# GpSimd ops that wait for the VectorE op ahead of them on a shared SBUF access, in a windowed attention and MLP kernel

## The chip, the cores and the metric

The kernel runs on one core of one Trainium2 chip. The metric is the device time of one execution in microseconds (us), as the median of a few runs. The names in this text: PE is TensorE (PEld its weight loads), DVE is VectorE, ACT is ScalarE, POOL is GpSimd, SP is the engine that issues the DMAs. "L399" is line 399 of the kernel file.

## The reference

Attention over 4 batches, 8 heads, 768 positions of 64 elements, in which a query sees the first 8 keys and the 96 keys up to itself, with a slope per head on the distance. Its output, 3072 tokens of 512, goes through a two-layer network with a cosine gate. All is float32.

```python
scores = scale * np.matmul(q, k.transpose(0, 1, 3, 2)) - slopes * dist
scores = np.where(keep, scores, -1000000000.0)      # keep: is_global | is_local
a = np.exp(scores - np.max(scores, axis=-1, keepdims=True))
a = a / (np.sum(a, axis=-1, keepdims=True) + 1e-09)
x = np.matmul(a, v)                                 # then heads side by side: 3072 x 512
h = x @ w_in                                        # 512 -> 2048
return (h * np.cos(h)) @ w_out                      # 2048 -> 512
```

The network's two weights arrive as float64, so the kernel gets them as pairs of 32-bit words and makes float32 of them itself.

## The kernel before

**Tiling.** The tokens are cut into 8 chunks of 384 (half a batch). A chunk's attention is done in 4 units of two heads (`plan_unit`, `plan_values`): scores on PE (L521 in the first 8 units, L525 later), a masked fold (L538) and the minimum of each row (L547) on DVE, the exponentials on ACT (L572), sums and reciprocals on DVE (L580, L583), the normalisation (`norm`, L595 and L600) on DVE or POOL, transposes on PE (L664), masking on the way out of PSUM on DVE (L672, L677), the product with the values on PE (L699). The result is split into a high and a low part, xh (L253 on ACT or L255 on DVE, the helper `copy`) and xl (L720, DVE).

**The network.** It goes in steps of 128 of the 2048 hidden columns (`plan_step`): PE multiplies by a block of w_in (L735, three products for the high and low parts), ACT and DVE make h cos h in four ops that hand on to each other (L752 ACT, L755 DVE, L758 ACT, L793 DVE), the result is split into gh (`copy`) and gl (L802, DVE or POOL), and PE multiplies by a block of w_out (L746). Two PSUM banks take turns for the first product.

**The weights.** Each of the 32 blocks of 128 x 512 weights goes through six ops (`plan_weights`): `wlow` (L378 on ACT, L380 on DVE or POOL), `wsign` (L385 on DVE, L388 on POOL), `wbias` (L394 ACT, L396 DVE or POOL), `wjoin` (L399, DVE only), `whigh` (`copy`: L253 ACT, L255 DVE, L257 POOL) and `wrest` (L409, DVE or POOL). The first 8 blocks of each weight are wanted for the first chunk, the others for the second (`PHASES`). Their raw words stay in tiles of their own; the joined words pass through two tiles `wu`.

**The order.** `Plan.run` goes through time with a cost in ns for each op on each engine it may run on, and picks an engine and a place in its queue. Ops with `port=True` on DVE, and every op on POOL, share one access to SBUF in this plan: `self.port` is the time until which it is taken, and the plan starts no second op on it before that. So in the plan's own times a POOL op and a marked DVE op are never under way together. What the plan gives out is a list of ops by start, and `emit` writes them into the engines' queues in that list's order. What each instruction waits for on the chip is what its data and buffers ask, and its own queue.

```python
holds = lambda o, x: x == POOL or (x == DVE and o.port)
...
if held and holds(o, e):
    continue
```

Until 45 us of the plan's time `emit` also fills PE's gaps with products of zeros (L1039).

Of the kernel before, what the change touches and what calls it, by code (L numbers as in the profile page):

```python
# [40 lines left out]
PE, ACT, DVE, POOL, SP = "PE", "ACT", "DVE", "POOL", "SP"  # L41
# [34 lines left out]
class Op:  # L76
    def __init__(self, engines, emit, after, uses, due, table, extra, port, mode):
        self.engines, self.emit, self.uses, self.due, self.table = engines, emit, uses, due, table
        self.extra, self.port, self.mode = extra, port, mode
        self.after = [a for a in after if a is not None]  # L80
        self.then = []
        self.left = len(self.after)
        self.ready = 0
        self.start = None


class Plan:
# [17 lines left out]
    def op(self, engines, emit, after=(), uses=(), due=None, table=None, extra=0, port=False, mode=None):  # L105
        o = Op(engines, emit, after, list(uses), due, table, extra, port, mode)
        for a in o.after:
            a.then.append(o)
        for u in o.uses:
            u.users += 1  # L110
        self.ops.append(o)
        return o
# [120 lines left out]
class Net:  # L233
# [789 lines left out]
    def emit(self, ops, banks):  # L1023

        nc = self.nc
        held = {b: [] for b in banks}
        for u in {id(u): u for o in ops for u in o.uses if u.at in held}.values():
            held[u.at].append((u.begin, u.end))
        last = 0
        for o in ops:  # L1030
            if o.engine == PE and o.start < FILL_TO:
                each = FILL_EACH if last > FILL_COLD else 2 * FILL_EACH
                n = int((o.start - last - FILL_REST) / each) if last else FILL_FIRST
                free = [b for b in banks if all(y < last or x > o.start for x, y in held[b])]
                if n > 0 and free:
                    ps = self.psum.tile([P, 512], F32, name="idle", tag=free[0])
                    wide = self.zeros.rearrange("p (o w) -> p o w", o=1).broadcast_to([P, 4, P])
                    for _ in range(n):
                        nc.tensor.matmul(ps, self.zeros, wide, start=True, stop=True)  # L1039
                last = o.start + o.engines[PE]  # L1040
            o.emit(o.engine)


def build(tc, *args):
# [54 lines left out]
```

## Time and profile before

| | |
|---|---|
| median of 3 runs | 712.63 us (712.12 to 714.5) |
| the profiled execution, its own time | 714.17 us |
| its span, first to last instruction | 712.4 us |
| PE busy | 688.6 us, 97% |
| DVE busy | 518.8 us, 73% |
| ACT busy | 450.9 us, 63% |
| POOL busy | 135.8 us, 19%, 166 instructions |
| mean granted clock of PE | 0.991 |

A share here is a mean over unlike stretches: PE's gaps lie almost all in the first 57 us and in the last 10, and POOL's work lies almost all in the first 160 us, where it makes the weights. The timeline gives each instruction's start and duration, and in brackets the idle time before it and what ended it.

### The profile page before, as it was taken

The page shows a single profiled execution, that of the slowest core. Times are in us where ns is not written, and L with a number is a line of the kernel's source. Part 1 is how long each engine was busy: PE and PEld are TensorE (multiplying, and loading weights), DVE is VectorE, ACT ScalarE, POOL GpSimd, SP SyncE. Part 2 cuts the span into 40 slices and gives each one's busy share as a digit, 9 for nine tenths or more (in the row PEclk, how much of TensorE's full clock was granted, in tenths as well). Part 3 has the DMA queues.
Part 4 walks back from the last instruction along what each step waited for, and adds up shares of the span by engine and source line. Part 5 has one row for each costly group of instructions (what it writes and reads, how often), then busy time and mean ns, then how long its engine had stood idle before and what let it go on. Part 6 is the DMA issues. An engine that isn't in the chain of part 4 may idle for free.

```text
span 712.4 us, 12947 instructions
## 1 busy us (share of the span) xinstructions
PE 688.6 (97%) x4483; PEld 598.4 (84%) x4483; DVE 518.8 (73%) x1542; ACT 450.9 (63%) x1130; POOL 135.8 (19%) x166
## 2 busy tenths in 40 slices
PE   7898999999999999999999999999999999999996
PEld 3657878988888888889889898888888888899884
DVE  7999999898767778487775887667785877743332
ACT  5799977786756576466664667566764666634342
POOL 4715656530002121011000121011000112000000
PEclk8999999999999999999999999999999999999999
DMA  8997210022420322132230422203122310001001
GB/s 303 407 351 209 59 48 24 1 59 64 112 68 29 83 65 65 48 103 60 56 71 15 112 61 58 59 19 106 42 68 67 90 49 2 1 1 45 1 0 50
DMA packets 32603, 55.74 MB, mean 78 GB/s; under 512 B 3472, under 2 KB 18192, under 8 KB 32528
## 3 DMA queue, kind: packets, MB, share of 16 engines
q1 hardware_dynamic: 32528, 54.82, 26.4%
q8 instruction: 37, 0.61, 0.4%
q14 instruction: 38, 0.31, 0.1%
HBM read 48.52 MB, written 6.29 MB: 77 GB/s over the span
## 4 chain that ended last, share of the span: by engine, by line
PE 72%; DVE 11%; ACT 8%; issue 2%; DMA 1%; POOL 0%; ACTq 0%; DVEq 0%; POOLq 0%; SPq 0%
PE bank L735 31%; PE bank L746 30%; PE bank L699 5%; PE bank L525 3%; ACT tt L572 2%; PE bank L664 2%; DVE wu L399 1%; ACT rr L758 1%; ACT L572 1%; DVE w L409 1%; DVE tt L547 1%; DVE gl L802 1%; DVE rr L755 1%; DVE qs L623 1%; DMA raw<-in_qk_dram 1%
## 5 line engine op out<-in xcount | busy, mean ns | idle before, releaser
L735 PE MATMUL bank<-xh,w 128*128 128x384 f32 x1024 | 298.1, 343 | 4.3 <-DVE rr L793 4.3
L746 PE MATMUL bank<-w,gh 128*128 128x512 f32 x768 | 243.6, 398 | 0.0
L735 PEld LDWEIGHTS bank<-xh,w 128*128 128x128 f32 x1024 | 189.1, 189 | 12.0 <-DVE rr L793 5.8
L735 PE MATMUL bank<-xl,w 128*128 128x384 f32 x512 | 173.3, 339 | 0.8 <-DVE xl L720 0.8
L746 PEld LDWEIGHTS bank<-w,gh 128*128 128x128 f32 x768 | 138.4, 188 | 21.5 <-ACT raw L394 0.3
L746 PE MATMUL bank<-w,gl 128*128 128x512 f32 x384 | 151.9, 396 | 0.0
L755 DVE SCALAR_TENSOR_TENSOR rr<-rr,bank 128x384 f32<-128x384 int32 x129 | 69.8, 542 | 102.6 <-ACT rr L752 102.2
L752 ACT ACTIVATE rr<-bank 128x384 int32<-128x384 f32 x129 | 62.1, 482 | 127.5 <-PE bank L735 124.5
L758 ACT ACTIVATE rr<-rr,half_pi 128x384 f32<-128x384 f32 x129 | 78.4, 613 | 43.0 <-DVE rr L755 41.4
L735 PEld LDWEIGHTS bank<-xl,w 128*128 128x128 f32 x512 | 96.8, 189 | 5.4 <-DVE xl L720 1.4
L793 DVE TENSOR_TENSOR rr<-bank,rr 128x384 f32<-128x384 f32 x129 | 70.5, 551 | 41.2 <-ACT rr L758 40.6
L572 ACT ACTIVATE tt<-tt,st 96x104 f32<-96x104 f32 (+1 forms) x256 | 94.2, 369 | 7.0 <-DVE st L547 6.4
L746 PEld LDWEIGHTS bank<-w,gl 128*128 128x128 f32 x384 | 72.1, 188 | 16.7
L257 POOL TENSOR_SCALAR ks<-raw 128x408 fp32r<-128x408 f32 (+1 forms) x35 | 21.1, 602 | 308.6 <-PE bank L525 291.6
L802 DVE TENSOR_TENSOR gl<-rr,gh 128x384 fp32r<-128x384 f32 (+1 forms) x113 | 65.9, 583 | 7.7 <-ACT gh L253 5.5
L253 ACT CAST gh<-rr 128x384 fp32r<-128x384 f32 (+1 forms) x99 | 50.2, 508 | 29.0 <-DVE rr L793 20.5
L547 DVE CUSTOM_DVE_ANT_0 tt<-bank,dd 96x104 f32<-96x104 f32 (+1 forms) x256 | 55.7, 257 | 3.0
L699 PEld LDWEIGHTS bank<-pv,v 104*64 104x64 f32 (+1 forms) x960 | 42.1, 138 | 12.5 <-issue 8.0
L525 PEld LDWEIGHTS bank<-ks,qs 128*96 128x96 f32 x384 | 45.8, 162 | 5.3 <-issue 0.8
L699 PE MATMUL bank<-pv,v 104*64 104x96 f32 (+1 forms) x960 | 48.3, 252 | 0.8 <-DMA raw<-in_qk_dram 0.4
L525 PE MATMUL bank<-ks,qs 128*96 128x200 f32 (+1 forms) x384 | 47.9, 255 | 0.5 <-DVE st L547 0.5
L572 ACT ACTIVATION_READ_ACCUMULATOR tt<-tt,st 96x1 f32 x256 | 47.9, 187 | 0.0
(96 smaller groups left out, 727.0 us busy)
## 6 DMA issues: line engine op xcount, KB each, us to landing
raw<-in_qk_dram SPq DMA_DIRECT2D x48, 224.0 KB
raw<-in_qk_dram SPq DMA_DIRECT2D x48, 198.0 KB
raw<-in_w_in_dram SPq DMA_DIRECT2D x16, 512.0 KB
raw<-in_w_out_dram SPq DMA_DIRECT2D x16, 512.0 KB
out_dram<-oo SPq DMA_DIRECT2D x24, 256.0 KB
v<-in_v_dram SPq DMA_DIRECT2D x16, 240.0 KB
v<-in_v_dram SPq DMA_DIRECT2D x16, 192.0 KB
raw<-in_qk_dram SPq DMA_DIRECT2D x4, 448.0 KB
```

Of the source, the lines that this page charges most:

```text
L253: self.nc.scalar.copy(out, x)
L525: nc.tensor.matmul(out, qs[:, m, q0], ks[:, k : k + w], start=m == 0, stop=m == 1)
L547: nc.vector.tensor_tensor_reduce(tt[t // 2].tile[:, t % 2, j, :w], ps.tile[:R, i * WIN : i * WIN + w], self.dd[:, v, :w], op0=ALU.add, op1 ...
L572: nc.scalar.activation(x, x, AF.Exp, bias=st.tile[:, c : c + 1], scale=-1.0, accum_out=st.tile[:, n2 + c : n2 + c + 1])
L699: nc.tensor.matmul(px.tile[j * D : (j + 1) * D, t * R : (t + 1) * R], vs.tile[:k, t + c, hs][:, j * D : (j + 1) * D], pv[:k, c, o : o + R] ...
L735: self.nc.tensor.matmul(ph[:, :CW], self.wi[f][:, w, kk * P : (kk + 1) * P], xx[:, kk, :], start=kk == 0 and m == 0, stop=kk == self.NK - ...
L746: self.nc.tensor.matmul(po, gg[:, ts], self.wo[f][:, w, :], start=start and m == 0, stop=stop and m == 2)
L752: self.nc.scalar.activation(r.bitcast(I32), ph, AF.Copy, scale=1.0 / TWO_PI, bias=0.25)
L755: self.nc.vector.scalar_tensor_tensor(r, r.bitcast(I32), -TWO_PI, ph, op0=ALU.mult, op1=ALU.add)
L758: self.nc.scalar.activation(r, r, AF.Sin, bias=self.half_pi)
L793: {DVE: dve}, lambda e, r=r, h=h: nc.vector.tensor_tensor(r(), h(), r(), op=ALU.mult), [o], [ph, rr]
L802: self.eng(e).tensor_tensor(g[1][:, cs], r(), g[0].bitcast(F32)[:, cs], op=ALU.subtract)
```

## The change

`emit` keeps the last instruction of the last DVE op with `port=True`, and the next POOL op in the list gets a wait on it. Each such DVE op is waited for at most once: a second POOL op right behind gets no wait of its own, but stands behind the first in POOL's queue. DVE never waits for POOL because of this change. The `norm`, `krest`, `low`, `wlow`, `wsign`, `wbias`, `whigh` and `wrest` ops on POOL are touched.

```diff
+        held_by = None
+        behind = mybir.DependencyInfo(mybir.DependencyClass.Sync, mybir.DependencyReason.SCHED_ONLY)
         for o in ops:
...
+            new = len(nc.cur_bb.bb.instructions)
             o.emit(o.engine)
+            if o.engine in (DVE, POOL):
+                engine = self.eng(o.engine).engine
+                new = [i for i in nc.cur_bb.bb.instructions[new:] if i.engine == engine]
+                if o.engine == DVE and o.port:
+                    held_by = new[-1]
+                elif o.engine == POOL and held_by is not None:
+                    self.tc.add_manual_dep(new[0], held_by.name, behind, reason="port")
+                    held_by = None
```

No instruction changes its place in any queue. What differs is the waits. POOL's queue at the start of the program, from the first scaling of queries (`raw_158`) on; `DVE_49` is DVE's semaphore, `DMAHW…` those of the loads:

```order
-L490 TENSOR_SCALAR raw_158<-raw_158,steep_104 128x384 [waits DMAHW3_49]
-L380 TENSOR_SCALAR raw_120<-raw_120 128x512 [waits DMAHW1_49]
+L490 TENSOR_SCALAR raw_158<-raw_158,steep_104 128x384 [waits DMAHW3_49,DVE_49]
+L380 TENSOR_SCALAR raw_120<-raw_120 128x512 [waits DMAHW1_49,DVE_49]
 L388 TENSOR_SCALAR raw_120<-raw_120 128x512 [waits Pool_49]
 L595 TENSOR_TENSOR tt_258<-tt_258,st_259 96x2x96 [waits DVE_49,Activation_49]
 L595 TENSOR_TENSOR tt_258<-tt_258,st_259 96x208 [waits Activation_49]
-L388 TENSOR_SCALAR raw_122<-raw_122 128x512 [waits DMAHW3_49,Activation_49]
+L388 TENSOR_SCALAR raw_122<-raw_122 128x512 [waits DMAHW3_49,DVE_49,Activation_49]
 L380 TENSOR_SCALAR raw_124<-raw_124 128x512 [waits DMAHW4_49]
 L490 TENSOR_SCALAR raw_229<-raw_229,steep_104 128x384 [waits DMAHW6_49,PE_49]
```

The first `wlow` and the next block's `wsign` now wait for DVE; the ops between keep their waits.

POOL's queue a little later, the weights' blocks that it reaches between 28 and 51 us:

```order
-L388 TENSOR_SCALAR raw_121<-raw_121 128x512 [waits DMAHW7_49]
+L388 TENSOR_SCALAR raw_121<-raw_121 128x512 [waits DMAHW7_49,DVE_49]
 L388 TENSOR_SCALAR raw_128<-raw_128 128x512 [waits DMAHW1_49,Activation_49]
-L380 TENSOR_SCALAR raw_131<-raw_131 128x512 [waits DMAHW1_49]
-L380 TENSOR_SCALAR raw_133<-raw_133 128x512 [waits DMAHW2_49]
-L388 TENSOR_SCALAR raw_130<-raw_130 128x512 [waits DMAHW3_49,Activation_49]
-L409 TENSOR_TENSOR w_759<-wu_755,w_759 128x512 [waits Activation_49]
+L380 TENSOR_SCALAR raw_131<-raw_131 128x512 [waits DMAHW1_49,DVE_49]
+L380 TENSOR_SCALAR raw_133<-raw_133 128x512 [waits DMAHW2_49,DVE_49]
+L388 TENSOR_SCALAR raw_130<-raw_130 128x512 [waits DMAHW3_49,DVE_49]
+L409 TENSOR_TENSOR w_759<-wu_755,w_759 128x512 [waits DVE_49,Activation_49,Pool_49]
```

Each of these but one has got a wait for DVE of its own; where that wait implies an older one, the older one is gone.

The same queue where the second half of the weights is made, some 120 to 135 us into the run:

```order
-L388 TENSOR_SCALAR raw_150<-raw_150 128x512 [waits DMAHW4_49]
-L409 TENSOR_TENSOR w_1594<-wu_1585,w_1594 128x512 [waits Activation_49]
-L388 TENSOR_SCALAR raw_145<-raw_145 128x512
-L409 TENSOR_TENSOR w_1640<-wu_1633,w_1640 128x512 [waits Activation_49]
-L388 TENSOR_SCALAR raw_147<-raw_147 128x512 [waits DMAHW7_49]
+L388 TENSOR_SCALAR raw_150<-raw_150 128x512 [waits DMAHW4_49,DVE_49]
+L409 TENSOR_TENSOR w_1594<-wu_1585,w_1594 128x512 [waits Activation_49,Pool_49]
+L388 TENSOR_SCALAR raw_145<-raw_145 128x512 [waits DVE_49]
+L409 TENSOR_TENSOR w_1640<-wu_1633,w_1640 128x512 [waits Activation_49,Pool_49]
+L388 TENSOR_SCALAR raw_147<-raw_147 128x512 [waits DMAHW7_49,DVE_49]
```

A `wsign` here waited for nothing but its data, long there; it now waits for DVE.

Which DVE op each waits for is told by the count in the built program. 65 of POOL's ops wait for a later DVE op than before. Laid on the trace of before, 45 of these 65 started there before that DVE op had ended: 9 of them in the first 57 us, 23 from 57 to 160 us, 13 later. The ones that matter most, with times of the trace of before:

| POOL op, its start | the DVE op it now waits for, its end |
|---|---|
| L380 at 11.27 | L600, 13.71 |
| L388 at 18.88 | L600, 20.38 |
| L388 at 21.59 | L399, 27.00 |
| L388 at 28.11 | L385, 36.94 |
| L380 at 31.28 | L399, 40.87 |
| L380 at 32.55 | L409, 43.16 |
| L388 at 33.28 | L399, 47.42 |
| L632 at 80.66 | L583, 83.26 |
| L632 at 97.40 | L399, 101.97 |
| L388 at 99.54 | L399, 104.48 |
| L409 at 109.17 | L255, 110.87 |
| L388 at 111.93 | L409, 115.25 |
| L802 at 313.50 | L623, 314.97 |

## Rows read from the trace of the kernel before

**Rows 1.** The page, part 1: busy time, share of the span and instructions.
```profile
PE 688.6 (97%) x4483; PEld 598.4 (84%) x4483; DVE 518.8 (73%) x1542; ACT 450.9 (63%) x1130; POOL 135.8 (19%) x166
```
**Rows 2.** Busy time by stretch: length, each engine's busy us, PE's granted clock, DMA share.
```profile
20.00:57.00 37.00, 30.30 (x243) 19.24 (x242) 36.10 (x125) 33.58 (x99) 17.02 (x18) 1.00 1.04 379
57.00:160.00 103.00, 100.55 (x650) 86.73 (x651) 94.36 (x224) 82.70 (x186) 57.57 (x47) 0.98 0.22 55
14.00:18.00 4.00, 4.00 (x21) 2.04 (x22) 3.47 (x20) 2.58 (x9) 0.09 (x1) 0.50 1.03 407
```
**Rows 3.** Timeline of PE: start, duration of the row, idle before and what ended it.
```profile
13.86 0.85 PE L664 MATMUL bank<-ident,tt 96*104 96x96 f32 x4 [1.08 <-DVE tt L600]
...
35.03 0.57 PE L664 MATMUL bank<-ident,tt 96*96 96x96 f32 x4 [1.34 <-ACT raw L378]
...
56.84 0.44 PE L735 MATMUL bank<-xh,w 128*128 128x384 f32 x1 [3.70 <-DVE rr L793]
...
102.49 0.44 PE L735 MATMUL bank<-xl,w 128*128 128x384 f32 x1 [0.83 <-DVE xl L720]
...
114.24 0.44 PE L735 MATMUL bank<-xh,w 128*128 128x384 f32 x1 [0.63 <-DVE rr L793]
...
316.42 1.39 PE L699 MATMUL bank<-pv,v 96*64 96x96 f32 x28 [0.41 <-DVE pv L677]
```
**Rows 4.** Timeline of DVE in the first 57 us.
```profile
11.26 1.08 DVE L595 TENSOR_TENSOR tt<-tt,st 96x192 f32<-96x192 f32 x2
12.27 1.44 DVE L600 TENSOR_TENSOR tt<-tt,st 96x416 f32<-96x416 f32 x1
...
17.36 0.16 DVE L580 TENSOR_SCALAR st<-st 96x8 f32<-96x8 f32 x1
...
18.63 1.75 DVE L600 TENSOR_TENSOR tt<-tt,st 96x416 f32<-96x416 f32 x1
20.68 0.56 DVE L720 TENSOR_TENSOR xl<-bank,xh 128x384 fp32r<-128x384 f32 x1 [0.30 <-ACT xh L253]
...
23.80 0.67 DVE L580 TENSOR_SCALAR st<-st 96x8 f32<-96x8 f32 x1
...
25.27 0.64 DVE L595 TENSOR_TENSOR tt<-tt,st 96x192 f32<-96x192 f32 x2
25.82 0.58 DVE L600 TENSOR_TENSOR tt<-tt,st 96x416 f32<-96x416 f32 x1
26.32 0.68 DVE L399 SCALAR_TENSOR_TENSOR wu<-raw 128x512 uint32<-128x512 uint32 x1
...
29.72 0.55 DVE L672 TENSOR_TENSOR pv<-bank,others 104x384 f32<-104x384 f32 x1
...
32.66 1.09 DVE L399 SCALAR_TENSOR_TENSOR wu<-raw 128x512 uint32<-128x512 uint32 x1
33.67 1.50 DVE L595 TENSOR_TENSOR tt<-tt,st 96x192 f32<-96x192 f32 x2
...
36.20 0.74 DVE L385 TENSOR_SCALAR raw<-raw 128x512 uint16<-128x512 uint16 x1
```
**Rows 5.** Timeline of POOL.
```profile
12.20 1.33 POOL L388 TENSOR_SCALAR raw<-raw 128x512 bf16<-128x512 bf16 x1
...
28.11 2.50 POOL L388 TENSOR_SCALAR raw<-raw 128x512 bf16<-128x512 bf16 x2
...
33.28 1.66 POOL L388 TENSOR_SCALAR raw<-raw 128x512 bf16<-128x512 bf16 x1
...
83.41 0.88 POOL L600 TENSOR_TENSOR tt<-tt,st 96x416 f32<-96x416 f32 x1 [1.68 <-DVE st L583]
```
**Rows 6.** Timeline of ACT, the `wbias` behind the `wsign` at 28.11.
```profile
38.11 0.67 ACT L394 ACTIVATE raw<-raw 128x512 f32<-128x512 f32 x1
```
**Rows 7.** Timeline of DVE from 97 to 115 us.
```profile
99.80 1.57 DVE L409 TENSOR_TENSOR w<-wu,w 128x512 fp32r<-128x512 f32 x1
...
112.16 1.56 DVE L399 SCALAR_TENSOR_TENSOR wu<-raw 128x512 uint32<-128x512 uint32 x1
```

## The prediction, made before the changed kernel ran

> **What bounds the kernel now.** Read the page's first part first [rows 1]: PE is busy 97% of the span, so at most some 24 us of PE's time can be won at all, and POOL, the one engine whose instructions change, is busy 19%. Then look where PE stands idle, by stretches [rows 2]. From 57 to 160 us PE idles 103 - 100.55 = 2.45 us. Before 57 us it waits much more, and part of what it does there is products of zeros. In that early stretch DVE is the full engine: 36.10 of 37 us from 20 to 57. So the time until PE runs without gaps is set by how fast DVE gets through its queue, and from then on by PE itself. Last, the timeline of PE [rows 3] says what ends its gaps: 3.70 us before 56.84, after which it is dense, and smaller ones at 13.86, 35.03, 102.49, 114.24 and 316.42. DVE stands behind all of them. The 1.34 us before 35.03 are put down to an old ACT op, but the two L595 there write what that transpose reads, so I take them as the cause.
>
> What has POOL to do with it? The same DVE op is long where a POOL op is under way and short where none is [rows 4]: L600 takes 0.58 us at 25.82, and 1.44 at 12.27 beside POOL's L388 of 12.20 [rows 5]; the two L595 take 0.64 together at 25.27, and 1.08 and 1.50 beside POOL; L399 takes 0.68 at 26.32 and 1.09 at 32.66. Ops that read PSUM don't care: L672 at 29.72 takes 0.55 in the middle of the two L388 of 28.11. POOL is there at that moment only because it runs ahead of the plan, by up to 14 us (the L388 at 33.28, for which the wait would end at 47.42).
>
> **The change part by part.** No instruction is added to an engine's work and none moves in a queue, DMAs included; POOL issues none. What is added is waits on POOL.
>
> *Startup, what DVE gets back.* In the first 57 us, the ops of POOL that moved leave these DVE ops alone: L595 at 11.26, 1.08 - 0.64 = 0.44; L600 at 12.27, 1.44 - 0.58 = 0.86; L580 at 23.80, 0.67 - 0.16 (as at 17.36) = 0.51; L399 at 32.66, 1.09 - 0.68 = 0.41; L595 at 33.67, 1.50 - 0.64 = 0.86. Sum 3.08 us. The L600 at 18.63 is long too (1.75), but the DVE op of 20.68 waited 0.30 us for ACT, which waits for PE: what L600 gains there only lengthens that wait, so I count nothing; it is the upper bound, 1.75 - 0.58 = 1.17 more. Do the moved POOL ops hit other DVE ops instead? After most of the DVE ops waited for, DVE's queue has PSUM work for longer than POOL needs; one L380 (behind the L409 that ends at 43.16) has less room than it needs. Its price lies between 0 and the 0.41 that an L380 cost L399 at 32.66; I take the middle, 0.2. So DVE arrives 2.9 us earlier where PE becomes dense; the lower bound is 0.
>
> *Startup, who waits for the late POOL ops.* The L388 that now waits until 36.94 ends 1.33 us later at 38.27; the `wbias` L394 that needs it started at 38.11 [rows 6]. It slips by some 0.2 us on ACT, and DVE reads it later still. The L388 of 21.59 has three ops behind it in POOL's queue; they all start after 27.00, and even at 1.33 us each the four end by 32.32, before the L399 of 32.66 that reuses a buffer of theirs. Both hold because DVE's own place in the plan is what POOL waits for; I charge nothing.
>
> *From 57 us on.* PE is dense, so only its gaps count. The 0.83 us before 102.49 wait for an L720 that stands behind an L409 of 1.57 us [rows 7] (0.68 by L399, another two-input op of the same size); the 0.63 before 114.24 for an L793 behind an L399 of 1.56. Both are longer by more than the gap, and the POOL ops beside them (99.54, 111.93) now wait. I take both gaps as gone: 1.46 us. At 313.50 POOL's L802 starts just ahead of L623, and the 0.41 us before 316.42 follow; the pattern comes once more 167 us later, so 0.82. Lower bound 0 for each; upper bound the 2.45 us of the whole stretch and these.
>
> *A cost.* The normalisation L600 of POOL at 83.41 now stands behind an L632 that waits for 83.26 and takes 1.06; it starts about 84.4 in place of 83.41, and a transpose on PE wants it. Price between 0 and 1.0; I take 0.3, since PE has other work queued ahead of that transpose.
>
> *Sum.* 2.9 + 1.46 + 0.82 - 0.3 = 4.9 us. The profiled execution took 714.17 us (span 712.4), so 709.3 for such a one; it lies 1.54 above the median, so **707.7 us** against 712.63. A measurement of this kernel can tell about 0.3% (2.1 us) from no change.
>
> *A rule against it.* In the row, L600 (12.27 to 13.71) ends 0.18 us after the L388 beside it (12.20 to 13.53) and takes 0.58 alone, so it is held for most of L388's time and not for all of it. The Trainium skill (SBUF — State Buffer, section "SBUF: two separate sides") says that VectorE and GpSimd share a port pair as an exclusive lock, and that whichever starts first has it while the other blocks fully. The trace agrees in kind, not in the full length. By that rule alone a wait ahead of the lock wins nothing if the next DVE op needs it too; that is the first rival.
>
> **The rivals.**
>
> *The block moves on.* POOL, released by the end of a DVE op, takes the access at once, and the next DVE op that needs it stands as long as before. For it: DVE does not wait for POOL, and behind L409 at 43.16 the room is short. Against it: the startup's blocks sit on L600, L595 and L399, and the op after these is PSUM work. It would give 0 of the 4.9: 712.6, or 711 with a third of the gain.
>
> *POOL's lateness reaches the path.* ACT's queue stops at each L394 whose L388 now comes 1.4 us after a DVE op, and with it the exponentials, L752 and L758 that stand behind. Place: the L394 of 38.11 and its like; I find 7 spots where the trace's slack is used up, at 0.2 to 0.7 us each, 2.2 us together. It decides as soon as DVE's own gain is under 2.2 us, so that these no longer move earlier with DVE. With nothing gained, 714.17 + 2.2 - 1.54 = 714.8: slower. For it: L394 stands almost exactly a POOL op's length behind in 11 places. Against it: ACT is busy 82.7 of 103 us from 57 to 160 [rows 2], so that most slips go into its idle time.
>
> *The clock.* From 14 to 18 us PE runs at 0.50 of its clock, its 1.2 GHz level [rows 2], right after the gaps that end at 13.86. If shorter gaps there keep it at 2.4 GHz, those 4 us of work take 2, and up to 2.0 us more are won: 705.7. The chain from there to ACT's xh runs over PE, so they would count.
>
> *It does nothing.* The dependency is named as one for scheduling only; but the queue's list shows the waits, so this is nearly excluded: 712.6.
>
> **How the numbers follow.** The forecast, 705.8 to 710.4, has 60%: the startup term is read from five rows that all agree. The clock's extra gain has 10%, the block that moves on 17%, lateness on the path 11%, nothing 2%. Faster by over 0.3% (below 710.5): 60 + 10 = 70%. Within: 17 + 2 = 19%. Slower: 11%. The range must leave out 20% at most: I let go most of the 11% at 714.8, and the tails of the clock case and of the first rival, and give 705.0 to 712.8. The forecast's own range is 705.8 to 710.4.
>
> **What would show it.** In the profile after: L600 near 12.3 takes about 0.6 us, and L580, L399 and L595 up to 35 us are as short as alone; PE's first dense row comes near 54 us in place of 56.84; the gaps of 0.83, 0.63 and 0.41 are gone; POOL's largest waits name DVE. Wrong would be: long DVE ops in new places (the block moved on), ACT idle ahead of L394 by more than 0.3 us in many places (lateness), or DVE short as said and PE dense no earlier, which would mean that ACT or PE, not DVE, sets the startup.

## The result and the profile after

The changed kernel takes 707.07 us (median of 4 runs, 707.03 to 707.61) beside 712.38 for the kernel before on the same chip: ratio 0.9922, 95% interval 0.9901 to 0.9942. Two further comparisons on the way gave 0.9916 (0.9898 to 0.9934) and 0.9920 (0.9902 to 0.9939). The forecast was 707.7 in a range of 705.0 to 712.8.

The page's first part, and two stretches of the table of busy time, answering to [rows 1, 2]:

```profile
PE 686.5 (97%) x4483; PEld 597.4 (85%) x4483; DVE 507.6 (72%) x1542; ACT 451.2 (64%) x1130; POOL 129.1 (18%) x166
```
```profile
20.00:57.00 37.00, 32.02 (x244) 21.85 (x242) 35.62 (x129) 35.31 (x104) 15.38 (x17) 0.95 1.04 381
57.00:160.00 103.00, 102.26 (x676) 88.81 (x675) 92.09 (x235) 85.10 (x194) 54.61 (x46) 1.00 0.23 60
```

DVE does the same 1542 instructions in 11.2 us less. From 57 to 160 us PE now idles 0.74 us in place of 2.45.

The timeline of DVE after, answering to [rows 4]:

```profile
11.06 0.64 DVE L595 TENSOR_TENSOR tt<-tt,st 96x192 f32<-96x192 f32 x2
11.62 0.58 DVE L600 TENSOR_TENSOR tt<-tt,st 96x416 f32<-96x416 f32 x1
...
17.12 0.75 DVE L600 TENSOR_TENSOR tt<-tt,st 96x416 f32<-96x416 f32 x1
19.17 0.56 DVE L720 TENSOR_TENSOR xl<-bank,xh 128x384 fp32r<-128x384 f32 x1 [1.30 <-ACT xh L253]
...
22.30 0.17 DVE L580 TENSOR_SCALAR st<-st 96x8 f32<-96x8 f32 x1 [0.61 <-ACT tt L572]
...
30.20 0.65 DVE L399 SCALAR_TENSOR_TENSOR wu<-raw 128x512 uint32<-128x512 uint32 x1
30.77 0.63 DVE L595 TENSOR_TENSOR tt<-tt,st 96x192 f32<-96x192 f32 x2
...
39.88 0.80 DVE L399 SCALAR_TENSOR_TENSOR wu<-raw 128x512 uint32<-128x512 uint32 x1
...
105.37 1.51 DVE L802 TENSOR_TENSOR gl<-rr,gh 128x384 fp32r<-128x384 f32 x1
```

The first two rows were 1.08 and 1.44 us before; L580, L399 and the second pair of L595 were 0.67, 1.09 and 1.50. L580, L399 and the L595 pairs are now as short as alone, and so is the first L600. The L600 at 17.12 gained too (1.75 to 0.75), and the idle time behind it grew from 0.30 to 1.30. The last row is a DVE op that is long in the new kernel; it comes back below.

The timeline of POOL after:

```profile
12.29 0.66 POOL L380 TENSOR_SCALAR raw<-raw 128x512 int32<-128x512 uint32 x1 [3.82 <-DVE tt L600]
...
33.27 2.55 POOL L388 TENSOR_SCALAR raw<-raw 128x512 bf16<-128x512 bf16 x2 [3.92 <-DVE raw L385]
...
79.01 1.07 POOL L632 TENSOR_TENSOR ks<-raw,ks 64x408 fp32r<-64x408 f32 x1 [2.70 <-DVE st L583]
80.15 0.88 POOL L600 TENSOR_TENSOR tt<-tt,st 96x416 f32<-96x416 f32 x1
...
105.17 1.30 POOL L409 TENSOR_TENSOR w<-wu,w 128x512 fp32r<-128x512 f32 x1 [3.10 <-DVE gh L255]
```

The brackets name the DVE op that POOL was released by: L600 at 12.29, L385 at 33.27, as the list in the section on the change says. The timeline of PE after, answering to [rows 3]:

```profile
31.72 0.84 PE L664 MATMUL bank<-ident,tt 96*96 96x96 f32 x8
...
53.21 0.69 PE L735 MATMUL bank<-xh,w 128*128 128x384 f32 x1 [3.70 <-DVE rr L793]
...
81.08 0.54 PE L664 MATMUL bank<-ident,tt 96*104 96x96 f32 x4 [0.30 <-POOL tt L600]
...
97.19 0.44 PE L735 MATMUL bank<-xl,w 128*128 128x384 f32 x1
...
442.18 1.05 PE L664 MATMUL bank<-ident,tt 96*104 96x96 f32 x8 [0.56 <-POOL tt L600]
```

PE becomes dense at 53.21 in place of 56.84; the product of 102.49 stands at 97.19 without its gap. Two gaps are new or larger, and POOL's L600 ends both. PE runs the same 4483 rows in both traces, so the start of one and the same instruction can be laid side by side:

| PE's instruction, start before and after | lead | change of the lead since the row above |
|---|---|---|
| L735, 56.84 and 53.21 | 3.63 | +3.63, startup |
| L521, 84.84 and 80.46 | 4.38 | +0.75 |
| L664, 85.10 and 81.08 | 4.01 | -0.37, POOL's L600 late |
| L735, 114.24 and 108.39 | 5.85 | +1.84, the gaps of 0.83 and 0.63 |
| L525, 158.46 and 151.76 | 6.71 | +0.86, gaps of 0.41 and 0.53 |
| L699, 316.42 and 309.27 | 7.15 | +0.44 |
| L664, 448.87 and 442.18 | 6.68 | -0.47 |
| L699, 483.22 and 476.06 | 7.17 | +0.49 |

The end keeps it: spans of 712.4 and 705.4. Between these two executions lie 7.1 us; between the medians 5.3, since the profiled execution of the kernel before was one of its longer ones.

### The profile page after: what moved, and what is told of

Read it like the earlier page. It is cut to its first block, busy times and chain, and to the rows that moved or that the text cites. A ratio compares the mean times of both kernels' runs of the same rounds, so it can differ in the third digit from the quotient of the medians.

```text
span 705.4 us, 12976 instructions
## 1 busy us (share of the span) xinstructions
PE 686.5 (97%) x4483; PEld 597.4 (85%) x4483; DVE 507.6 (72%) x1542; ACT 451.2 (64%) x1130; POOL 129.1 (18%) x166
## 5 line engine op out<-in xcount | busy, mean ns | idle before, releaser
L735 PE MATMUL bank<-xh,w 128*128 128x384 f32 x1024 | 298.1, 343 | 3.9 <-DVE rr L793 3.9
L746 PE MATMUL bank<-w,gh 128*128 128x512 f32 x768 | 243.5, 398 | 0.0
L735 PEld LDWEIGHTS bank<-xh,w 128*128 128x128 f32 x1024 | 188.9, 189 | 11.6 <-DVE rr L793 5.1
L735 PE MATMUL bank<-xl,w 128*128 128x384 f32 x512 | 173.2, 338 | 0.0
L746 PEld LDWEIGHTS bank<-w,gh 128*128 128x128 f32 x768 | 138.4, 188 | 21.5 <-ACT rr L752 0.3
L746 PE MATMUL bank<-w,gl 128*128 128x512 f32 x384 | 152.0, 396 | 0.0
L735 PEld LDWEIGHTS bank<-xl,w 128*128 128x128 f32 x512 | 96.8, 189 | 4.6 <-DVE xl L720 0.4
L746 PEld LDWEIGHTS bank<-w,gl 128*128 128x128 f32 x384 | 72.1, 188 | 16.7
L802 DVE TENSOR_TENSOR gl<-rr,gh 128x384 fp32r<-128x384 f32 (+1 forms) x113 | 66.3, 587 | 8.0 <-ACT gh L253 5.6
L699 PEld LDWEIGHTS bank<-pv,v 104*64 104x64 f32 (+1 forms) x960 | 42.1, 138 | 11.4 <-issue 7.0
L525 PEld LDWEIGHTS bank<-ks,qs 128*96 128x96 f32 x384 | 45.8, 162 | 4.8 <-issue 0.3
L699 PE MATMUL bank<-pv,v 104*64 104x96 f32 (+1 forms) x960 | 48.2, 252 | 0.0
L525 PE MATMUL bank<-ks,qs 128*96 128x200 f32 (+1 forms) x384 | 47.9, 255 | 0.1
```

Source lines behind the costliest of these rows:

```text
L525: nc.tensor.matmul(out, qs[:, m, q0], ks[:, k : k + w], start=m == 0, stop=m == 1)
L699: nc.tensor.matmul(px.tile[j * D : (j + 1) * D, t * R : (t + 1) * R], vs.tile[:k, t + c, hs][:, j * D : (j + 1) * D], pv[:k, c, o : o + R] ...
L735: self.nc.tensor.matmul(ph[:, :CW], self.wi[f][:, w, kk * P : (kk + 1) * P], xx[:, kk, :], start=kk == 0 and m == 0, stop=kk == self.NK - ...
L746: self.nc.tensor.matmul(po, gg[:, ts], self.wo[f][:, w, :], start=start and m == 0, stop=stop and m == 2)
L802: self.eng(e).tensor_tensor(g[1][:, cs], r(), g[0].bitcast(F32)[:, cs], op=ALU.subtract)
```

## The experiments

Theory: a DVE op that shares the access stands while a POOL op is under way; the waits move POOL's ops to where DVE reads PSUM, and the end gains what DVE's queue gains in the startup, and later what PE's gaps lose. Rivals: only the startup counts, or only the later waits; or the place is of no account, as long as POOL no longer runs ahead. Ratios are to the kernel before in the same comparison; they are of the means of the runs, so they differ a little from a quotient of the medians.

### The two halves

The waits on the first 22 POOL ops of the plan alone (the other half has `nth > 22`):

```diff
-                elif o.engine == POOL and held_by is not None:
+                elif o.engine == POOL:
+                    nth += 1
+                    if held_by is not None and nth <= 22:
```

> The waits stand only on the plan's first 22 GpSimd ops (up to 56 us); the later ones run free as before. My theory (two separate gains: DVE ops no longer prolonged in the startup, and short gaps of PE after 57 us): PE's dense start stays near 53.2 us, the gaps of 0.83 us near 99 and 0.63 near 111 come back, and the median lies at 709.0, between 708.3 and 710.2, some 2 us above the changed kernel and 3.4 below the one before. Rival A (only the later waits matter, the startup's lead being eaten later): 711.5 or more. Rival B (the startup alone is the gain, later gaps are chance): 707.5 or less.

> The complement: no waits on the first 22 GpSimd ops, waits on all later ones. My theory: PE's dense start is back at 56.8 us with L600 at 12.3 long again (1.4 us), the gaps near 102.5 and 114 are gone or short, median 710.6, between 709.8 and 711.4; the gains of this and of the startup alone add up to that of the whole within 0.7 us. Rival A (later waits are what matters): 707.5 or less. Rival B (startup alone): 712 or more.

Measured: the startup alone 0.9953 (0.9937 to 0.997), median 709.66, 3.4 us less; the rest alone 0.9957 (0.994 to 0.9975), median 709.36, 3.1 less and below the range that was expected. Together 6.4, beside 5.8 of the whole (three ratios, mean 0.9919, of 712.5): additive within the expected 0.7, and the rivals fall. With the later waits off, PE's gaps are back:

```profile
98.38 0.44 PE L735 MATMUL bank<-xl,w 128*128 128x384 f32 x1 [1.06 <-DVE xl L720]
...
110.11 0.45 PE L735 MATMUL bank<-xh,w 128*128 128x384 f32 x1 [0.62 <-DVE rr L793]
```

The second half gained more than the 1.8 expected. The startup can't be the reason, since both kernels have no waits there; but 3.1 is near the 7.17 - 3.63 = 3.5 us that PE's lead gained behind the startup in the table above, so the expectation was too low. The profiled execution of this half also shows how the startup comes out by chance. DVE there, then POOL, without waits:

```profile
11.02 0.63 DVE L595 TENSOR_TENSOR tt<-tt,st 96x192 f32<-96x192 f32 x2
11.58 1.03 DVE L600 TENSOR_TENSOR tt<-tt,st 96x416 f32<-96x416 f32 x1
```
```profile
11.45 0.72 POOL L380 TENSOR_SCALAR raw<-raw 128x512 int32<-128x512 uint32 x1 [3.15 <-DMA raw<-in_w_in_dram]
```

The load that frees L380 landed 0.2 us later and DVE was 0.2 us earlier than in [rows 4, 5]: the L595 got through, and only L600 was caught. PE was dense from 54.88. In the trace of before it was 56.84. Without waits the startup is a matter of such chances. Over all comparisons the kernel before lies between 709.8 and 715.0 (61 runs), the changed one between 706.4 and 708.0 (16 runs).

### One collision put back

The changed kernel without the wait on the L380 of 11.27:

```diff
-                elif o.engine == POOL and held_by is not None:
-                    self.tc.add_manual_dep(new[0], held_by.name, behind, reason="port")
+                elif o.engine == POOL:
+                    nth += 1
+                    if held_by is not None and nth != 2:
+                        self.tc.add_manual_dep(new[0], held_by.name, behind, reason="port")
                     held_by = None
```

> The changed kernel without one wait: the L380 of GpSimd that started at 11.27 us before the change is free again, and the L388 behind it. If my first two startup terms (0.44 + 0.86 us for the L595 and L600 beside them) reach the path, these two are long again (1.1 and 1.4 us), PE's rows near 24.5 us come 1.0 to 1.4 us later than in the changed kernel, and the median is 0.8 to 1.4 us above it (ratio 0.992 to 0.994). Rival (the idle time of VectorE near 19 us, where it waits for ACT, takes such a delay up): PE's rows at 24.5 and the median as in the changed kernel.

Measured: 0.9941 (0.9918 to 0.9964), 708.68 beside 706.77 for the changed kernel in the same comparison, 1.9 us lost; beside its other two medians (707.07 and 707.13) it is 1.6. DVE and POOL:

```profile
11.42 1.91 DVE L595 TENSOR_TENSOR tt<-tt,st 96x192 f32<-96x192 f32 x2
13.26 0.58 DVE L600 TENSOR_TENSOR tt<-tt,st 96x416 f32<-96x416 f32 x1
```
```profile
11.33 0.64 POOL L380 TENSOR_SCALAR raw<-raw 128x512 int32<-128x512 uint32 x1 [3.01 <-DMA raw<-in_w_in_dram]
12.05 1.33 POOL L388 TENSOR_SCALAR raw<-raw 128x512 bf16<-128x512 bf16 x1
```

The two DVE groups are 1.27 us longer than alone (1.91 + 0.58 - 0.64 - 0.58), which is the 0.44 + 0.86 of the prediction, this time all on the L595. Against the profile of the changed kernel shown above, PE's L664 of 31.72 comes at 33.33, and the span is 707.0 beside 705.4: 1.6 later at both. Of these, 1.27 are the collision; 0.36 were there before it, since DVE's L595 starts at 11.42 in place of 11.06, and DVE's rows lie 0.36 later from 7.7 us on, where no op is long yet. So one wait is worth some 1.3 to 1.6 us, about a quarter of the whole gain, and the rival falls: the idle time near 19 us is 1.30 in both profiles and doesn't take it up. Against the profile of the changed kernel from the same comparison the L664 comes 3.0 later, not 1.6, and the end 2.2; PE's clock is low for a shorter time there in the startup, to which the point on the clock below comes back.

### Released one op, and two ops, too early

```diff
                 if o.engine == DVE and o.port:
-                    held_by = new[-1]
-                elif o.engine == POOL and held_by is not None:
-                    self.tc.add_manual_dep(new[0], held_by.name, behind, reason="port")
-                    held_by = None
+                    before, held_by = held_by or before, new[-1]
+                elif o.engine == POOL and before is not None:
+                    self.tc.add_manual_dep(new[0], before.name, behind, reason="port")
+                    before = None
```

> Each GpSimd op is released one VectorE op too early: by the port op ahead of the one the plan puts last before it, so that it meets that last one. My theory (what counts is that the op does not run beside a VectorE op that uses the access): L600 near 12 us is again 1.2 to 1.5 us long, the startup loses 1.5 to 3 of its 3.6 us, median 709.5, between 708.5 and 711.0. Rival (it is enough that GpSimd no longer runs far ahead; a microsecond earlier or later does not matter): 707.5 or less.

Measured: 0.9895 (0.987 to 0.992), 705.46 beside 713.72. My expectation was wrong, and the time is that of the rival, or better. The comparison was made again beside the changed kernel:

> The changed kernel itself once more, on the same chip as the variants beside it. By the first comparison (0.9922 of the kernel before) it should lie 5 to 6 us below the kernel before. If the lead of the release one op too early (0.9895 against 0.9922, intervals that overlap) is real, this kernel's ratio stays at 0.991 or above; if that lead was chance, it falls to 0.990 or below.

> The changed kernel once more, as the reference of a square of four on one chip: released after the last port op or one early, zeros until 45 or until 50 us of the plan. Ratio 0.990 to 0.993, as in both comparisons before (0.9922 and 0.9916).

> The release one port op too early again, beside the changed kernel on the same chip. Theory: its lead comes from the gaps of PE that it does without (0.30 near 80.8, 0.19 near 101 and 0.56 near 441 us, 1.05 together), so it lies 0.7 to 1.6 us below the changed kernel. Rival (its better ratio was chance): within 0.4 us.

Measured: the changed kernel 0.9916 and 0.9920, as given above (706.77 and 707.13); one early again 0.9894 (0.9873 to 0.9914), 705.36 beside the 707.13. That is a lead of 1.8 us, a little more than the 0.7 to 1.6 expected. In the first comparison the ratios put it at 1.9 (0.9895 beside 0.9922, not measured side by side); the intervals overlap both times. DVE in this second run of one early, then POOL:

```profile
11.01 0.64 DVE L595 TENSOR_TENSOR tt<-tt,st 96x192 f32<-96x192 f32 x2
11.57 0.58 DVE L600 TENSOR_TENSOR tt<-tt,st 96x416 f32<-96x416 f32 x1
...
16.73 1.75 DVE L600 TENSOR_TENSOR tt<-tt,st 96x416 f32<-96x416 f32 x1
18.40 0.54 DVE L720 TENSOR_TENSOR xl<-bank,xh 128x384 fp32r<-128x384 f32 x1
```
```profile
11.73 0.95 POOL L380 TENSOR_SCALAR raw<-raw 128x512 int32<-128x512 uint32 x1 [3.43 <-DVE tt L595]
...
16.00 0.99 POOL L595 TENSOR_TENSOR tt<-tt,st 96x192 f32<-96x192 f32 x2 [1.90 <-DVE worst L563]
16.96 1.34 POOL L388 TENSOR_SCALAR raw<-raw 128x512 bf16<-128x512 bf16 x1
```

POOL's L380 is released by the L595, and starts at 11.73, 0.16 us after DVE's L600. L600 keeps its 0.58 us; it is L380 that is long, 0.95 in place of 0.66. So the op that comes first keeps the access, and one too early is just late enough: DVE's L600 starts at 11.57 without idle time, POOL 0.08 us after the L595 has ended (11.65). POOL then stands behind L600, and goes on without a further wait. The fourteen traces together bear this out for DVE. Of its ops with two inputs from SBUF (L595, L600, L399, L409, L632, L802) that overlap a POOL op by over 0.1 us, 155 start ahead of it, and none of these is more than 0.15 us longer than the short ones of its shape; 320 start while a POOL op is under way, and 236 of these are. Of the other 84, 28 have a POOL op beside them that ends within 0.45 us; in 56 the POOL op is the long one, though it started first. So a start ahead kept the access for DVE each time, and for POOL in most cases.

The second L600 is one of them. It starts at 16.73, while POOL's L595 pair is under way until 16.99, and POOL's L388 follows that pair at 16.96 without a break: L600 stands through both and is 1.75 long, as it was at 18.63 before. A DVE op that stands did not get in between two POOL ops that follow at once. Here it costs next to nothing. L720 behind it starts at 18.40, about 0.5 us later than in the profiles of the two repeats of the changed kernel (17.83 and 17.88), and PE's L521 at 25.52 starts where it does there (25.48 and 25.53).

DVE's prolonged time (each op's duration over the lower quartile of its shape, where that is more than 0.1 us) is 7.8 us here, 11.6 in the changed kernel, 24.6 before. The three gaps of 0.30, 0.19 and 0.56 us that POOL's lateness or DVE cost the changed kernel near 81, 101 and 442 us are gone but for 0.20 of the last; that is 0.85 of the 1.8 us. What the rest is made of is open.

Whether earlier still is better:

```diff
+                    ports, held_by = ports[-2:] + [new[-1]], new[-1]
...
+                    self.tc.add_manual_dep(new[0], ports[0].name, behind, reason="port")
```

> GpSimd is released two port ops of VectorE too early, where the run before released it one too early and lost nothing. My theory now (the op that starts first has the access and the later one stands; released one op early, GpSimd comes just after VectorE's last port op has started, because VectorE goes on at once and GpSimd needs some 0.1 to 0.2 us for its wait, and it then goes on without that delay): two early, it gets in between the last two wherever the second does not follow at once, so that VectorE's prolonged time, 7.8 us with one early and 24.6 in the kernel before, rises to 10 to 18, and the time lies 1 to 4 us above the one of one early: ratio 0.991 to 0.995. Rival (the earlier the better as long as GpSimd does not run far ahead): ratio 0.989 or less.

Measured: 0.9994 (0.9978 to 1.001), 712.9: the whole gain is lost, more than I expected. DVE's prolonged time is 19.8 us, and the startup is that of before, row for row [rows 4]:

```profile
11.22 1.09 DVE L595 TENSOR_TENSOR tt<-tt,st 96x192 f32<-96x192 f32 x2
12.23 1.44 DVE L600 TENSOR_TENSOR tt<-tt,st 96x416 f32<-96x416 f32 x1
```
```profile
11.33 0.76 POOL L380 TENSOR_SCALAR raw<-raw 128x512 int32<-128x512 uint32 x1 [3.14 <-DVE st L547]
12.16 1.33 POOL L388 TENSOR_SCALAR raw<-raw 128x512 bf16<-128x512 bf16 x1
```

L380 starts at 11.33, as it did in the run without its wait: the release two ops back comes no later than its load did there. So "POOL no longer far ahead" is not enough, and the point of release decides within one DVE op. Part of the loss may come through PE's clock: seven of the twelve executions had a mean granted clock of 0.986, where the kernel before has 0.988 to 0.994 in this comparison, and took 712.86 to 715.08; the three at 0.992 and 0.993 took 710.29 to 711.07. What is cause there and what follows is not shown.

### The wait in both directions

```diff
                 if o.engine == DVE and o.port:
                     held_by = new[-1]
+                    if pool is not None:
+                        self.tc.add_manual_dep(new[0], pool.name, behind, reason="port")
+                        pool = None
                 elif o.engine == POOL ...
+                    pool = new[-1]
```

> The changed kernel, and the same rule the other way round as well: a VectorE op that uses the access waits for the last GpSimd op that the plan puts ahead of it. My theory (after the change VectorE runs in time with the plan and GpSimd's ops stand in its room, and where they meet VectorE is held anyway): between 706.5 and 709, most likely 707.8, because a few GpSimd ops that wait for a transfer or for ACT now hold VectorE as well; the later VectorE ops of 1.2 to 1.6 us beside a GpSimd op become short and stand idle in their place. Rival (meetings cost VectorE more than waiting does, as each is slowed beyond the other's length): 705.5 or less.

Measured: 0.9978 (0.9963 to 0.9992), 711.15. No DVE op is prolonged any more (page: DVE 496.5 us busy), and yet it lies 3 us above the expected middle and some 4 above the changed kernel (0.9978 beside 0.9919). The list of waits (us in total, times, longest) has what DVE now waits for, and PE has larger gaps:

```profile
DVE gl L802 <- POOL w L409: 2.7, 3, 1.1
DVE gl L802 <- POOL raw L388: 2.5, 3, 1.0
```
```profile
136.22 0.58 PE L525 MATMUL bank<-ks,qs 128*96 128x200 f32 x4 [0.91 <-DVE st L547]
...
142.37 0.57 PE L664 MATMUL bank<-ident,tt 96*96 96x96 f32 x4 [0.82 <-ACT w L253]
```

DVE's idle time that POOL ended adds up to 23.5 us in this profile and to 2.7 in the changed kernel's; the prolonged time that went was 11.6. So here standing at the access cost DVE less than the waits in its queue do. Taking all collisions away is not what wins.

### Zeros in the gap ahead of the dense part

In the profiles the granted clock falls to 0.50, PE's 1.2 GHz level, in the 3.7 us gap that ends at 53.21 or behind it. `emit` fills gaps with products of zeros until 45 us of the plan. With 50 us, 14 more come into that gap:

```diff
-FILL_TO, FILL_REST, FILL_EACH, FILL_FIRST, FILL_COLD = 45000, 150, 250, 10, 7000
+FILL_TO, FILL_REST, FILL_EACH, FILL_FIRST, FILL_COLD = 50000, 150, 250, 10, 7000
```

It was tried on the release one early, then on the changed kernel, and on the release one early again, with all four combinations of release and zeros in one comparison:

> The release one op early, and products of zeros until 50 us of the plan in place of 45, which puts 14 more of them (0.23 us each) into PE's gap of 3.7 us ahead of its dense start. In all profiles so far the granted clock falls to 0.50 in that gap or just behind it, for 3.4 or 6.8 us, of which PE works some 3 to 6. If the idle gap is what the fall follows on, the clock stays at 1.00 there, and the time falls by 1.4 to 3.0 us against the release one op early alone: ratio 0.985 to 0.9875. Rival A (the fall has another cause, or comes later instead): as one early alone, 0.9885 to 0.9905. Rival B (the zeros hold up the product behind them): 0.991 or more.

> The changed kernel with the 14 further products of zeros. Theory (idle PE is what the low clock follows on, and a low stretch of 3.4 us costs the end about 1 us): no granted clock of 0.50 within 45 to 65 us, 1 to 2 us below the changed kernel. Rival (the low clock only moves, or what PE wins there is lost behind it to VectorE): within 0.5 us of the changed kernel.

> Both together again. Theory: the two add up, 2 to 3 us below the changed kernel and 1 to 2 below the release one op early. Rival (the first comparison, 0.9886 against 0.9895, was right that the zeros bring next to nothing on top): within 0.7 us of the release one op early.

Measured: first 0.9886 (0.9867 to 0.9906), median 704.80, at the better end of the range of rival A and outside my own, though in that profile the low clock was gone. In the comparison of all four the changed kernel took 707.13, with the zeros 705.68 (0.9901, 0.9881 to 0.9921), one early 705.36, both 703.67 (0.9873, 0.9853 to 0.9892). The zeros win 1.5 and 1.7 us, one early 1.8 and 2.0. They add up, and both together win somewhat more than the expected 2 to 3. Busy time from 48 to 62 us of one early, then with the zeros (the eighth figure is the granted clock):

```profile
48.00:62.00 14.00, 10.29 (x41) 9.58 (x41) 11.16 (x32) 12.79 (x26) 6.89 (x8) 0.76 1.06 319
```
```profile
48.00:62.00 14.00, 13.31 (x91) 10.51 (x89) 13.18 (x33) 13.91 (x29) 8.34 (x9) 1.00 1.07 319
```

PE with the zeros:

```profile
47.75 3.19 PE L1043 MATMUL idle<-zeros 128*128 128x512 bf16 x14
...
51.63 0.45 PE L735 MATMUL bank<-xh,w 128*128 128x384 f32 x1 [0.69 <-DVE rr L793]
```

The dense part starts hardly earlier than with one early alone (51.63 and 51.75), but at the 2.4 GHz level. Both together are the best version here, 1.3% below the kernel before and 3.5 us below the changed one.

The zeros do not decide the clock in every execution. One of the five executions of one early without them has a mean granted clock of 0.996 and took 704.13, the other four 0.989 and 704.93 to 706.05; in the first run with the zeros two of five have 0.991 and took 704.80 and 704.93. The three profiles with zeros show no 0.50 between 20 and 690 us, all others do.

## Why the prediction was right, point by point

- **The startup, 2.9 us forecast.** Right in mechanism, somewhat small: 3.63 measured. The five ops became as short as alone, and one put back cost the 1.3 us of its two terms on DVE. Of the 0.73 too little, 0.49 is an op that the sum left out, the L580 of 31.86 beside POOL's L380 of 31.28, before and after:

```profile
31.86 0.65 DVE L580 TENSOR_SCALAR st<-st 96x8 f32<-96x8 f32 x1
```
```profile
29.89 0.16 DVE L580 TENSOR_SCALAR st<-st 96x8 f32<-96x8 f32 x1
```

  Another 0.20 is DVE's earlier arrival at the first L595 (11.06 for 11.26), which no wait explains. The term of 0.51 for L580 at 23.80 came out by luck: the L563 ahead of it was long too (0.64, and 0.15 after), so that DVE got 0.99 back, but half of it went into the 0.61 us for which L580 now waits for ACT. The L600 at 18.63 was rightly counted at nothing: the wait for ACT's xh took its 1.00 us. The new collision was at its place, the L399 behind the L380 of 39.48, with 0.12 (0.80 - 0.68) for the 0.2.
- **PE's gaps, 1.46 forecast.** Both went whole: the rows of 102.49 and 114.24 stand at 97.19 and 108.39 without idle time. A new gap of 0.19 came between them, before 101.30. PE's lead grew by 1.84 us there all the same; what is beyond the idle times is open. Two gaps that the sum left out, of 0.41 and 0.53 us near 146 and 158, shrank to 0.20 and vanished, and the lead grew by 0.86.
- **The pattern at 316 and 483, 0.82 forecast.** 0.44 + 0.49. With the later waits off both gaps stay (0.43 and 0.41).
- **The cost, 0.3 forecast.** A gap of 0.30 at 80.8, 0.37 of lead lost. A second like it near 442 us, 0.47, was not foreseen. It comes in every profile of a kernel with the later waits on the last port op alone (gaps of 0.55 to 0.57 us in six profiles), and not without them, with one early or with waits in both directions (0.19 to 0.25). In front of it a DVE L802 starts 0.47 us after the op that the trace names; why is open.
- **Lateness on the path.** The waits came, but not on the path. ACT's waits for these POOL ops rose from 1.8 us in all to 4.1, in six places, by about the 2.2 that the rival reckoned with. From the list of waits after:

```profile
ACT raw L394 <- POOL raw L388: 4.1, 6, 2.4
```

  PE's idle time fell all the same, from 2.45 to 0.74 us between 57 and 160, where ACT is busy 85.10 of 103.
- **The block moves on.** Not in the startup, but from 85 us on: beside POOL's L409 of 105.17, released by L255, the next DVE op L802 takes 1.51 us for its 0.56. PE had no gap there, so it cost little; released one early, less of it comes, and PE's gap near 101 goes. The Trainium skill (SBUF — State Buffer, section "SBUF: two separate sides") has it that the first of the two keeps the shared ports for its whole instruction. By that rule the second op stands whichever engine it is on, and both runs agree in kind: L802 stands behind L409 here, and L380 behind L600 (0.95 for 0.66) with one early. They differ in two things: L380 loses 0.29 of the 0.42 us for which it overlaps L600, not all of it; and the L600 of 16.73, which stood at POOL's L595 already, let a POOL op go first that started 0.23 us after it.
- **The clock.** The rival came in part, and was lost again. In the profile shown, PE is at 0.50 from 14 to 18 us as before, and the mean granted clock from 8 to 22 us is 0.76 in both. In the profiles of the two repeats of the changed kernel it is 0.88 there, and PE is dense at 51.92 and 51.91, 1.3 us earlier than 53.21. But the low clock then lasts longer at the dense start. From 48 to 62 us, the profile shown and the first repeat:

```profile
48.00:62.00 14.00, 10.30 (x48) 9.23 (x46) 12.13 (x34) 13.37 (x31) 8.15 (x8) 0.88 1.06 326
```
```profile
48.00:62.00 14.00, 10.28 (x41) 9.46 (x40) 11.16 (x32) 12.83 (x27) 6.93 (x8) 0.76 1.07 319
```

  Of the 1.3 us some 0.2 to 0.3 are left at PE's L746 of 66.11 (65.84 and 65.95), and the spans are 704.8 and 705.1 beside 705.4. So a startup won by the clock alone is worth little here; why the clock is lower for longer there is open. The zeros win at that place.
- **The sum.** 4.9 forecast for an execution like the profiled one, 7.1 between the two profiled ones. The median came out right, 707.7 against 707.07, and that is partly luck: I took the profiled execution's 1.54 us over its median off once more, and this made up for most of the 2.2 that the sum was short. That much of the excess was collisions, which went, is likely from the narrower spread (706.4 to 708.0 in place of 709.8 to 715.0), but not shown. Too small were the startup (0.7), the gaps left out (0.9), PE's lead past the two gaps (0.4) and between 57 and 84 us (0.75, which I had nothing for: 0.2 of it is there at 61 us, behind the stretch of low clock, and the rest comes in the L521 between 73 and 84); against it stands the 0.47 near 448. One step was wrong in its reason: I took "POOL beside a DVE op" as the harm. The harm is POOL ahead of it: with one early POOL's L380 is beside L600, and L600 keeps its 0.58.

## What to carry to other kernels

Where two engines share an access, don't only count how often their ops meet: look which starts first, and let the one on the path be it. In this kernel a wait on the op ahead of the last one did that somewhat better than a wait on the last, since POOL started 0.1 us after its release and DVE at once; one op further was already too early, so try the point of release in steps. A forecast against one profiled execution should ask what made it longer than the median, since the change may remove just that.

## What the runs showed of the hardware that was not expected

- A start 0.1 to 0.2 us earlier or later decides which engine stands: L600 takes 1.44 us beside an L388 that started 0.07 us ahead of it, and 0.58 beside an L380 that came 0.16 us after it and took 0.95 for 0.66.
- A DVE op that stands is passed by a second POOL op right behind the first: the L600 of 16.73 stood through POOL's L595 and L388, 1.75 us in all.
- Waits in both directions removed every prolonged op and were 4 us slower than waits in one: DVE waited 20.8 us more for POOL.
- 14 products of zeros in a 3.7 us gap kept the granted clock at 1.00 in the profile where it had been 0.76 over 14 us, and were worth 1.5 to 1.7 us of the whole in the comparison of all four.
